# Small edits to a sliding-window attention and long-convolution kernel: 16-bit sine reads, masks accumulated where they fall, another row order, copies by DMA

## The chip, the cores and the metric

One core of a Trainium2 chip. The metric is the device time of one execution in microseconds (us), as the median of several executions. The profiler's span, from first to last instruction, is some 1.8 us shorter than that time. A program on a single core has no second die to compare with, so a single run's state is judged only against other runs of the same kernel; all runs here were listed as fast, and only such runs are compared.

## The reference, cut to what matters

Four layers with residuals on x of 2048 positions by 512 channels, bf16: attention, long convolution, attention, convolution.

```python
def _A_ref(x, wqkv, wo):                 # H = 32 heads, Dh = 16, window W = 8, dilation 2
    idx  = pos[:, None] - off[None, :]   # off = 0, 2, ..., 14
    mask = idx >= 0
    logits = einsum("bhsd,bhswd->bhsw", q, k[idx]) * scale
    attn   = softmax(where(mask, logits, -1e9))
    return einsum("bhsw,bhswd->bhsd", attn, v[idx]) @ wo
def _B_ref(u, A, B, C, log_dt, Dskip):   # complex state of 128 per channel
    K = real(einsum("dn,dnl,dn->dl", C, exp(dt*A*l), dt*B))      # one filter per channel, length 2048
    return irfft(rfft(u) * rfft(K)) + u * Dskip
x = x + _A_ref(layernorm(x), ...)
x = x + _B_ref(layernorm(x), ...)        # and both once more
```

## The kernel before

It runs in stages, and engines are shared in each: power tables of exp(dt*A) and a table for B (DVE and ACT, to 60 us); tables for A, the filter products `pk` and the keys of layer 0 (60 to 130); logits of layer 0 (to 160); weighted sum of the values (to 223), in whose gaps the sine tables g and the permuted filter `k_perm` are made; first convolution (to 311); logits (to 349) and values (to 407) of the second attention; second convolution (to 465). The parts that matter here, with the names that the traces use: PE is TensorE, DVE VectorE, ACT ScalarE, POOL GpSimd; `A_pr` and `prod` are products of queries and keys for the logits, `ex` their exponential, `s` its sum over the window, `rs` the reciprocal of that sum, `attn` the weights, `pav` the products of weights and values, `po` their sum, `pq` a projection, and `pb` what the convolution's matmuls write. The schedule fixes the program's order for PE, DVE, ACT and the DMA queue, and not for GpSimd (`MAN` in the kernel):

```python
def linit(self, q):                       # a full mask ahead of the logits of four rows
    L = self.ps_l.tile([P, 4, W, H], F32, name="L")
    for j in range(2):
        nc.tensor.matmul(L[:, 2*j:2*j+2], lhsT=e0, rhs=maskrow[...512 columns...], start=True, stop=True)

for q, ft in slots:                       # logits; DVE multiplies, PE sums over channels
    mult(q, ft); ...; lsum(q, ft)
    if ft == 0 and q > 0: mx(q - 1); ...; sub_exp(q - 1)
    if ft == 1 and q > 0: recip(q - 1)    # DVE: sums s over ex; ACT: ln and exp
    if ft == 3 and q > 0: norm_p(q - 1)
for n in range(16):                       # values; events ("p", n) and ("o", n) carry side work
    pv_mult(n); ...; pv_sum(n); ...; out_proj(n - 1)

def build_g2(...):                        # sine tables g, four blocks h, two buffers
    def indices(h):                       # GpSimd
        gi[h] = tmp.tile([P, 2, 4, P], I32, name="g2_i", bufs=2)
        ... iota; tensor_scalar(gi[h][:, k], gi[h][:, k], p21, bias, mult, add)
    def wrap(h):                          # DVE: bitwise_and 8191
    def sines(h):                         # ACT Sin, then a DMA to g_dram
```

`k_part(h, j)` copies the filter from `k_rl` into `k_perm`; the DMA queue (SP) issues all loads and stores in program order. `v_ext` and `kT_ext` hold values and keys with a halo of earlier rows, which is copied from the block before, one partition down.

## Time and profile before

| | before |
|---|---|
| time, median of 3 | 467.31 us (466.93 to 468.07) |
| profiled span | 465.0 us |
| busy share PE / DVE / ACT | 77% / 87% / 71% |

The prediction shows the table by stage and the gaps that the change aims at. For the reading afterwards I use seven marks, each the start or end of one named group of instructions in the trace, so that a stage's length doesn't depend on how a window is cut: A, the last `pk` matmul ends; B, the first value product `pav` starts; C, the last output projection (`pq<-wop`) of layer 0 starts; D, the first `prod` of layer 1 starts; E, its first `pav`; F, the ten matmuls that keep PE warm before the second convolution start; and the end of the span.

### The profile page before, as it was taken

How to read it: one execution, taken by the hardware profiler on the slowest of the kernel's cores; microseconds unless marked ns; L12 is line 12 of the kernel's file. 1: busy time of each engine (PE TensorE's matmuls, PEld its weight loads, DVE VectorE, ACT ScalarE, POOL GpSimd, SP SyncE). 2: the span in 40 equal slices, each digit the busy share in tenths (PEclk: the TensorE clock that was granted, in tenths of full speed). 3: DMA queues.
4: the chain of work that ended last, by engine and by line, in shares of the span. 5: the costliest groups of instructions: out<-in, count | busy, mean ns of one | idle time of the engine just before them, and what ended most of it. 6: DMA issues, size and time to landing. Idle time of an engine off the chain costs nothing.

```text
span 465.0 us, 12705 instructions
## 1 busy us (share of the span) xinstructions
PE 359.3 (77%) x5463; PEld 269.0 (58%) x5500; DVE 405.1 (87%) x570; ACT 328.8 (71%) x548; POOL 35.1 (8%) x46
## 2 busy tenths in 40 slices
PE   1000064879899887999898898999997999996795
PEld 1000023566575565777687788555555787775784
DVE  7799996999989898899687988889889999879854
ACT  5999669675555436998799986774652669699833
POOL 2000103000070004100400000000000020000000
PEclk9999995999999989999999899999999999999989
DMA  8900810101111763282256540670022053116614
GB/s 217 391 13 2 89 45 1 43 10 22 50 16 27 196 218 99 70 313 120 92 206 234 201 162 23 171 239 1 2 80 80 3 204 161 38 56 207 204 47 137
DMA packets 57402, 52.21 MB, mean 112 GB/s; under 512 B 28829, under 2 KB 45826, under 8 KB 56066
## 3 DMA queue, kind: packets, MB, share of 16 engines
q1 hardware_dynamic: 57202, 51.27, 35.5%
q8 instruction: 43, 0.70, 0.7%
q10 hardware_dynamic: 144, 0.13, 0.2%
q14 instruction: 13, 0.11, 0.1%
HBM read 30.28 MB, written 13.24 MB: 94 GB/s over the span
## 4 chain that ended last, share of the span: by engine, by line
PE 50%; ACT 20%; DVE 16%; DMA 7%; issue 4%; SPq 2%; DVEq 0%; ACTq 0%
PE po L374 9%; PE pp L218 6%; PE pq L315 5%; PE pq L161 5%; PE pq L386 4%; PE L L271 4%; PE pk L1096 4%; DVE pav L366 3%; DVE t L746 3%; ACT a1s L684 3%; DMA kf_ring<-kf_dram 2%; PE pb L695 2%; ACT ws L1014 2%; ACT x_blk L135 2%; PE pb L702 2%
## 5 line engine op out<-in xcount | busy, mean ns | idle before, releaser
L366 DVE TENSOR_TENSOR pav<-attn,v_ext 128x4096 bf16<-128x4096 bf16 x32 | 72.8, 2283 | 0.0
L374 PE MATMUL po<-ident,pav 128*128 128x128 bf16 x1024 | 64.3, 222 | 5.0 <-DVE pav L366 4.8
L374 PEld LDWEIGHTS <-pav 128*128 128x128 bf16 x1024 | 60.3, 100 | 13.0 <-DVE pav L366 9.5
L264 DVE TENSOR_TENSOR prod<-qT,kT_ext 128x4096 bf16<-128x4096 bf16 x29 | 65.8, 2285 | 1.0 <-ACT qT L163 0.6
L204 PE MATMUL pt<-ident,x_blk 128*128 128x128 bf16 x64 | 5.6, 241 | 41.5 <-ACT x_blk L135 41.5
L780 PE MATMUL pb<-Wp,t 128*128 128x128 bf16 x256 | 31.8, 222 | 5.9 <-DVE t L746 4.8
L377 ACT CAST oT<-po 128x512 bf16<-128x512 f32 x32 | 18.6, 580 | 25.1 <-PE po L374 25.1
L1096 PE MATMUL pk<-B_t,A_t 128*64 128x84 bf16 (+1 forms) x512 | 25.4, 210 | 12.3 <-issue 9.3
L218 PE MATMUL pp<-xnT,kT_ext 128*128 128x512 bf16 x125 | 31.7, 396 | 3.9 <-ACT xnT L207 3.5
L271 PEld LDWEIGHTS <-prod 128*128 128x128 bf16 x928 | 27.2, 96 | 10.0 <-DVE prod L264 3.6
L765 ACT CAST ub<-pb 128x1024 bf16<-128x1024 f32 x32 | 31.8, 1040 | 1.1 <-DVE t L746 1.1
L781 PE MATMUL pb<-WpJ,t 128*128 128x128 bf16 x256 | 31.4, 222 | 1.5 <-DVE t L746 1.5
L1096 PEld LDWEIGHTS <-A_t 128*64 128x64 bf16 (+1 forms) x512 | 23.1, 110 | 15.6 <-issue 12.3
L702 PE MATMUL pb<-a1s,w_sb 128*128 128x64 bf16 x768 | 30.3, 197 | 1.9 <-ACT ub L765 1.4
L386 PE MATMUL pq<-wop,oT 128*128 128x512 bf16 x112 | 30.6, 388 | 0.8
L317 ACT CAST v_ext<-pq 128x512 bf16<-128x512 f32 x32 | 18.7, 586 | 15.8 <-PE pq L315 15.5
L315 PE MATMUL pq<-wv,xnT 128*128 128x512 bf16 x119 | 29.5, 379 | 0.4
L161 PE MATMUL pq<-xnT,kT_ext 128*128 128x512 bf16 x120 | 29.3, 379 | 0.5 <-issue 0.3
L702 PEld LDWEIGHTS <-w_sb 128*128 128x128 bf16 x768 | 26.6, 100 | 5.1 <-issue 2.5
L271 PE MATMUL L<-ind,prod 128*128 128x8 bf16 x928 | 27.5, 166 | 2.3 <-DVE prod L264 2.1
L204 PEld LDWEIGHTS <-x_blk 128*128 128x128 bf16 x64 | 4.5, 108 | 42.9 <-ACT x_blk L135 42.4
L684 ACT CAST a1s<-pb 128x1024 bf16<-128x1024 f32 x28 | 27.4, 1025 | 2.1 <-PE pb L695 1.9
(224 smaller groups left out, 869.7 us busy)
## 6 DMA issues: line engine op xcount, KB each, us to landing
w_sb<-w_dram SPq DMA_DIRECT2D x8, 1024.0 KB
w_dram<-w_zero SPq DMA_DIRECT2D x1, 4096.0 KB
kf_ring<-kf_dram SPq DMA_DIRECT2D x16, 256.0 KB
kf_ring<-kf_dram SPq DMA_DIRECT2D x32, 128.0 KB
v_ext<-v_ext SPq DMA_DIRECT2D x4, 784.0 KB
x_blk<-in_A_x_dram SPq DMA_DIRECT2D x4, 512.0 KB
kT_ext<-in_A_wqkv_dram SPq DMA_DIRECT2D x4, 512.0 KB
x_sb<-in_A_x_dram SPq DMA_DIRECT2D x4, 512.0 KB
```

What stands on the lines that cost most here:

```text
L161: nc.tensor.matmul(pq[:], lhsT=self.wqk[:, dt, ft * P:(ft + 1) * P], rhs=self.xnT[:, dt, q * 512:(q + 1) * 512], start=(dt == 0), stop=(dt ...
L218: nc.tensor.matmul(pp[:], lhsT=self.wqk[:, dt, D + ft * P: D + (ft + 1) * P], rhs=self.xnT[:, dt, b * 512:(b + 1) * 512], start=(dt == 0), ...
L264: nc.vector.tensor_tensor(pr, self.qT[q][:, ft].unsqueeze(1).to_broadcast([P, W, 4, P]), kap, ALU.mult)
L271: self.nc.tensor.matmul(L[:, al, w, ft * 8:(ft + 1) * 8], lhsT=pr[:, w, al, :], rhs=self.c["ind8"][:], start=False, stop=True, skip_group_ ...
L315: nc.tensor.matmul(pp[:], lhsT=xnT[:, dt, a * P:(a + 1) * P], rhs=wv[:, dt, :], start=(dt == 0), stop=(dt == NDT - 1))
L366: nc.vector.tensor_tensor(pv[:], attn[:, n % 4].unsqueeze(2).to_broadcast([P, W, DH, H]), vap, ALU.mult)
L374: nc.tensor.matmul(po[:, ft, :], lhsT=pvf[:, w, ft * P:(ft + 1) * P], rhs=ident[:], start=(w == 0 and ft == 0), stop=(w == W - 1), skip_gr ...
L386: nc.tensor.matmul(pw[:], lhsT=oT[:, ftp, :], rhs=wo[:, ftp, :], start=False, stop=(ftp == NDT - 1))
L684: (nc.scalar.copy if eng == "act" else nc.vector.tensor_copy)(dst, src)
L702: nc.tensor.matmul(p2[:, j, :], lhsT=self.w2[:, ec * EC + j, :], rhs=a1s[:, ec * EC + j, :], start=True, stop=True)
L765: nc.scalar.copy(ub[:], p2)
L1096: nc.tensor.matmul(o, lhsT=lhs, rhs=Bt[:, ri, c * CH + ql].rearrange("p b g -> p (b g)"), start=(not half and j % 4 == 0 and ri == 0), sto ...
```

## The change

It takes DVE and ACT work away (integer wraps before the sines, casts and copies that a DMA can do), gives each sine index table memory of its own so that GpSimd no longer waits for a buffer between two tables, and reorders: statistics of block 1 into an idle stretch of ACT, masks after the logits and only where they fall, the reciprocal one slot later, value row 2 ahead of row 1. The core of the diff:

```diff
@@ mask
-        for j in range(2):
-            nc.tensor.matmul(L[:, 2 * j:2 * j + 2], lhsT=self.c["e0"], rhs=...to_broadcast([1, 2, W, H]), start=True, stop=True)
+    def mask(self, q):                         # called after the last lsum of q
+            a = q * 4 + 2 * j; w0 = a // 2 + 1
+            if w0 < W: matmul(L[:, 2 * j:2 * j + 2, w0:], ..., start=False, stop=True)
@@ core
-            projs += [(v_proj, a) for a in vs[6:]] + [(q_proj, 3, 0), (q_proj, 3, 1)]
+            projs += [(v_proj, a) for a in vs[6:]]
-                if ft == 1 and q > 0:
+                if ft == 2 and q > 0:
                     recip(q - 1)
+            q_proj(3, 0); q_proj(3, 1)
+            rows = [0, 2, 1, *range(3, NA)]
-                if n in (0, 2, 4, 6):
+                if n in (1, 2, 4, 6):
                     mult(3, n // 2)
@@ key halos, powers
+        if ext == "dma":
+            for t in range(NDT):
+                nc.sync.dma_start(self.kT[:, t, e0:e1, 1:P], self.kT[:, t, e0 + 16:e1 + 16, 0:P - 1])
-                    nc.scalar.copy(Pw[:, :, k - 3, 3, :], cv[:, 1])
+                    nc.sync.dma_start(Pw[:, :, k - 3, 0, :], Pw[:, :, k - 3, 1, :])
@@ build_g2: full-scale 16-bit angles, low half read in place, no wraps, borrowed memory
-        gi[h] = tmp.tile([P, 2, 4, P], I32, name="g2_i", bufs=2)
-    def wrap(h): nc.vector.tensor_scalar(gi[h][:], gi[h][:], 8191, None, ALU.bitwise_and)
+    own = tmp.tile([P, 2, 8 * P], I32, name="g2_i")
+    gi = [own[:, 0], own[:, 1], *(room[:, (2 + h) * 16 * P:(3 + h) * 16 * P].bitcast(I32) for h in range(2))]
+        gs = room[:, h * 8 * P:(h + 1) * 8 * P]            # room is the k_perm tile, not yet filled
+        nc.scalar.activation(gs, low16(gi[h]), ACT.Sin, scale=s8)
@@ statistics of block 1
             ln_a(0, "act")
+            stats(1, "act")
...
             front(0)
-            stats(1, "act")
@@ events
-              ("m", 0, 3): [G(gx, 0), G(gx, 1)],
+              ("m", 0, 3): [G(gx, h) for h in range(4)],
```

Left out: the twiddle tables of the second kind, which get the same 16-bit reading, and DVE's small index operations, which move from the start into later gaps, and a few moves of single loads.

## The prediction

> **What bounds the kernel now.** I read the chain of waits by engine first, then a table of busy time by stage, then each engine's instructions in order of time with the idle time before them. The shares by engine, from the page:
>
> ```profile
> PE 50%; ACT 20%; DVE 16%; DMA 7%; issue 4%; SPq 2%; DVEq 0%; ACTq 0%
> ```
>
> No engine owns the span, so a saving must be judged by stage. The table has start:end, length, then busy us of PE, PEld, DVE, ACT, POOL, the granted clock, DMA share and GB/s:
>
> ```profile
> 0.00:60.00 60.00, 5.12 (x37) 3.65 (x38) 52.96 (x117) 49.18 (x81) 4.36 (x16) 1.00 0.55 138
> 60.00:124.00 64.00, 46.96 (x534) 30.99 (x536) 59.31 (x98) 46.56 (x84) 5.16 (x3) 0.92 0.12 31
> 124.00:160.00 36.00, 35.42 (x586) 23.59 (x592) 31.41 (x26) 19.48 (x33) 9.38 (x8) 1.00 0.25 61
> 160.00:223.00 63.00, 56.16 (x746) 43.04 (x751) 57.14 (x55) 44.55 (x94) 6.87 (x9) 0.95 0.50 163
> 310.00:350.00 40.00, 39.52 (x499) 22.62 (x507) 34.18 (x28) 22.18 (x40) 0.00 (x0) 1.00 0.17 49
> 350.00:410.00 60.00, 56.51 (x794) 43.09 (x800) 56.85 (x61) 37.44 (x91) 2.90 (x1) 1.00 0.28 101
> ```
>
> To 60 us (powers and B table) DVE and ACT are both nearly full; to 124 (A tables, products, keys) DVE again, with a PE/ACT chain; 124 to 160 and 310 to 350 (logits) are PE's; the value stages (160 to 223, 350 to 410) hold PE and DVE nearly level. The two long convolution stages (223 to 310, 410 to 465) are not touched. The gaps that the change aims at, in order of time:
>
> ```profile
> 23.06 0.63 ACT L1022 CAST pow_t<-sq_z 128x512 bf16<-128x512 f32 x1
> 42.67 0.69 DVE L594 TENSOR_SCALAR w_qi<-w_qi 128x1024 int32<-128x1024 int32 x1
> 56.05 2.93 ACT L135 ACTIVATE x_blk<-x_blk,ln_nb,ln_rstd 128x512 bf16<-128x512 bf16 x4 [3.47 <-DVE ln_nb L125]
> 72.40 0.16 DVE L110 SCALAR_TENSOR_TENSOR ln_msq<-ln_s 128x4 f32<-128x4 f32 x1 [2.69 <-ACT ln_junk L80]
> 153.70 0.42 DVE L343 TENSOR_TENSOR s<-ex 128x512 bf16<-128x512 bf16 x1 [2.19 <-ACT ex L337]
> 182.71 0.69 DVE L634 TENSOR_SCALAR g_i<-g_i 128x1024 int32<-128x1024 int32 x1 [1.38 <-POOL g_i L631]
> 182.40 1.06 ACT L638 ACTIVATE g_s<-g_i 128x1024 bf16<-128x1024 int32 x1 [2.61 <-DMA g_dram<-g_s]
> 329.55 0.42 DVE L343 TENSOR_TENSOR s<-ex 128x512 bf16<-128x512 bf16 x1 [2.14 <-ACT ex L337]
> ```
>
> And the DMA queue's own issues ahead of the first value rows:
>
> ```profile
> 130.65 18.11 SPq L1114 DMA_DIRECT2D kd_dram<-kgs  x24
> 152.06 0.60 SPq L410 DMA_DIRECT2D v_ext<-rows  x1
> 152.70 0.66 SPq L320 DMA_DIRECT2D v_ext<-v_ext  x1
> ```
>
> The even value rows are ready at 147.1 (the eighth v_ext cast), but their halo copy is issued at 152.70, since the queue is busy from 130.65 on. It lands at 158.9 in the chain; the first value product (pav) starts at 159.7.
>
> **What the Trainium skill says.** "ScalarE: Activation LUTs", section "What ACT_TABLE_LOAD costs", gives an ACTIVATE with immediate operands 186 ns + 0.833 ns per column, and about 93 ns of overlap back to back. For 512 columns that is 613 ns, some 0.52 us apart; the trace has 0.63 us and 0.51 to 0.53 us spacing, so it agrees, and each removed pow_t cast is worth 0.51 us of ACT. "SBUF — State Buffer", "SBUF: two separate sides", says that the port pair shared by VectorE and GpSimd is an exclusive lock. The trace shows only POOL stretched (its g_i pair takes 4.52, 2.88, 1.63 and 2.24 us), while DVE's 4096-column products beside it keep 2.28. So moving all index work early on POOL should not slow DVE. "TensorE: Matmul & The Clock Gate", Part 1, says PE drops to half clock after about 3.4 us of idleness. After a waiting stretch one po group of 32 here took 3.56 us instead of 1.96, so a PE bubble costs a little twice.
>
> **The change part by part.**
>
> *To 62 us.* The twenty small DVE operations between 4.77 and 7.17 us move away from the start. The first ws product then waits only for the transposed A_im and the exponential (both near 6.0), gain 1.15. They return later as 1.6 us inside a stretch without DVE gaps. The removed casts free 5 x 0.51 = 2.5 us of ACT, but DVE paces those steps (its work runs unbroken from 20.5 to 40.1), so this is not gained. ACT's index work before the tenth squaring, with the f_t pair now there, is 3.2 instead of 2.6 us, and I keep DVE's 0.8 us gap there. The bit masks go: 42.40 to 43.44, 1.04 us. Sum for DVE at 45 us: about -0.5; ACT about +0.4.
>
> *62 to 130 us.* Before, ACT idled 3.47 us before normalising block 0, then ran the statistics of block 1 (6.05 us) after its keys. Now these statistics fill the idle time. ACT: 47.0 + 5.9 + 6.05 puts block 0 at 58.95 instead of 56.05; + 11.07 for keys + 6.05 for block 2 gives block 1 normalised from 76.05 instead of 79.06, gain 3.0. DVE loses its gaps of 2.69 and 0.59 us and three halo copies (0.34 + 0.60 + 0.60), so it stays ahead. The chain from 79 to 123 alternates ACT and PE and keeps the 3.0. The two mask matmul pairs (1.02 us) and the 0.67 us wait for the last key eviction no longer stand before the last products, about 1.5 more. The last products end near 125.4 instead of 129.9: -4.5.
>
> *130 to 160 us.* Moving the reciprocal one slot later lets DVE skip its waits of 1.47 and 2.19 us, and two query projections (2 x 0.86) leave the path ahead of the last logits. But the halo copy of the even rows still follows 24 kd_dram issues and the wop loads: it comes 28.3 us after the last products, as before. So DVE could start at 151.5 and waits to about 154.5. Gain at the first pav: 5.2, not 8. Order 0, 2, 1, 3 keeps the odd copy (landing near 159.5) off the path, since row 1 comes third.
>
> *160 to 223 us.* DVE loses four wraps (4 x 0.60) and the waits for POOL (2 x 1.38) and for k_rl (0.20): 5.4 us. ACT's waits for the g_dram writes (2.61 + 0.73 + 0.23) go too, but lie beside that. PE's work is 16 x 2.87 for the rows + 3.2 logits + 1.7 projections + 0.9 = 51.7 us, DVE's now 53.7, and PE ends 4.6 after DVE's last product. So DVE's saving passes through: -10.6 at 213.
>
> *310 to 410 us.* The same reordering of the core, with no crowded DMA queue. DVE's gaps of 2.14 and 2.08 vanish, the last logits come 1.73 + 0.55 us earlier (projections, mask columns), then the maximum waits some 0.9 us for them: net -3.1. The masks shrink from 4096 to 1792 columns per layer; by their 0.53 us per pair that is about 1.0 us of PE, partly counted above.
>
> Sum: 467.3 - 10.6 - 3.1 = 453.6. I add 1.4 for coupling between three nearly full engines and half-clock PE after the new wait for v_ext: **455.0 us**.
>
> **The rivals.**
>
> *The DMA queue becomes the wall.* Some 17 more issues (5 powers, 12 key halos) go in order through one queue, each half a us or so. If the key halos of block 2, queued after 24 kd_dram issues, land late, DVE's first logits product waits. At that estimate they land near 118 to 120 against a DVE arrival of 117.3, while PE takes its logits only at 125, so it should be hidden. If v_ext is late as well, 4 us are given back: 459. For it: the v_ext reading above. Against it: nothing new stands between kd_dram and v_ext.
>
> *PE was the bound all along in the logits and value stages.* PE is 98% and 94% busy there, and removing DVE work then does nothing: only the K stage (4.5), the mask columns (2) and the moved projections count, some 458 to 460. For it: the chain is PE's from 207 to 223 and from 357 to 405. Against it: in 160 to 223 PE waited on DVE's pav and on x_sb (2.31 us), and DVE had no slack.
>
> *The statistics fill delays block 0.* Keys of block 0 come 2.9 us later; if the products are held by that instead of by ACT's later work, the K stage gains only about 1.5 and the total is 458.
>
> *Better than the sum.* If ACT's freed 2.5 us do shorten the power steps, and PE keeps up: 450.
>
> **Range and chances.** The rivals put the weak side at 458 to 460 and the strong side at 450; I set 449.5 to 460.5. The 2% line is 458.0. The sum lies 3 us under it after the correction, and two of the three adverse rivals cross it only together: faster 0.78, same 0.21, slower 0.01.
>
> **What would show it.** In the changed profile: no idle before ACT's first x_blk, and none near the second block's ln_msq; the last pk matmuls ending near 125; the first pav near 154.5, behind a v_ext landing rather than behind DVE work; no g_i wraps on DVE, and g_s sines without a DMA wait; the first pb near 213; DVE without waits for ex in both logits stages; layer 1 shorter by about 3 us from first logits to its first pb; the convolution stages unchanged within 0.5 us. The prediction is wrong if DVE waits for kT_ext halos or k_rl, if pav starts later than 157, or if PE's groups in the value stages slow down.

## The result, and the profile after

| | before | changed |
|---|---|---|
| time, median of 4 | 467.12 us (466.77 to 468.07) | 455.42 us (454.86 to 456.39) |
| ratio | | 0.9749 (95%: 0.9725 to 0.9773) |
| profiled span | 465.0 us | 453.2 us |

A ratio here is the mean time of one kernel's fast runs over that of the other's of the same rounds, so it isn't quite the ratio of the medians. The total is where it was predicted. Whether the steps are is another question, and the marks answer it. "Control" is the changed kernel once more, run beside the experiments; the predicted column takes the prediction's own steps.

| stage | before | changed | control | control less before | predicted |
|---|---|---|---|---|---|
| start to A (powers, tables, keys) | 129.87 | 126.28 | 124.95 | -4.9 | -4.5 |
| A to B (logits, layer 0) | 29.83 | 28.41 | 28.42 | -1.4 | -0.7 |
| B to C (values, layer 0) | 62.74 | 59.85 | 59.87 | -2.9 | -5.4 |
| C to D (convolution 1) | 88.89 | 89.17 | 88.83 | -0.1 | 0 |
| D to E (logits, layer 1) | 37.92 | 35.12 | 35.12 | -2.8 | -3.1 |
| E to F (values, layer 1) | 57.58 | 58.20 | 57.88 | +0.3 | 0 |
| F to the end (convolution 2) | 58.17 | 56.17 | 55.53 | -2.6 | 0 |

Two columns of one kernel differ too: the first stage by 1.3 us. The cause stands in the trace. Here is the second half of block 0's `pk` products in the changed kernel's first profile (start, us, engine, line, operation, names, shapes, count, idle before):

```profile
78.66 5.03 PE L1111 MATMUL pk<-B_t,A_t 128*128 128x84 bf16 x64 [0.60 <-ACT kgs L1115]
```

and in the control:

```profile
79.47 2.91 PE L1111 MATMUL pk<-B_t,A_t 128*128 128x84 bf16 x64 [1.36 <-ACT kgs L1115]
```

The same 64 matmuls of the same program run at nearly half speed in one execution and at full speed in the other: the granted clock was 0.50 over the first 5.03 us and 1.00 over the 2.91 us of the control. In the first profile PE had stood idle for 3.52 and 1.29 us ahead of the two groups before, in the control for 2.79 and 0.77; the sixth experiment's profile has 3.51 and 1.29 and 5.03 us again. Such stretches fall differently in each execution. The last stage, whose code no edit touches, took from 55.33 to 59.47 us in the runs below. Start, length, busy us of PE, PEld, DVE, ACT, POOL, clock, DMA share and GB/s of that stage, first in the control, then in the slowest of the runs (the seventh experiment):

```profile
395.07:450.60 55.53, 43.69 (x848) 39.07 (x847) 41.09 (x56) 39.37 (x46) 0.00 (x0) 0.97 0.44 137
```

```profile
396.83:456.30 59.47, 46.45 (x848) 41.45 (x847) 41.18 (x56) 39.37 (x46) 0.00 (x0) 0.91 0.42 128
```

DVE and ACT do the same work in the same time; PE is 2.8 us busier at a clock of 0.91. So the -2.6 of the last row is no gain of the change, and anything under 2 us is read from stage lengths that don't meet such stretches: A to B and D to E repeat to 0.02 us between profiles of the same code.

The stages of the changed kernel, cut as near as possible as before:

```profile
58.00:120.00 62.00, 48.42 (x538) 33.17 (x543) 58.48 (x97) 43.53 (x74) 4.74 (x3) 0.92 0.20 43
120.00:155.00 35.00, 34.68 (x597) 23.43 (x600) 34.44 (x26) 19.65 (x33) 25.16 (x16) 1.00 0.30 72
155.00:216.00 61.00, 56.05 (x773) 42.43 (x780) 56.53 (x54) 45.70 (x96) 2.67 (x4) 1.00 0.56 178
303.00:340.00 37.00, 36.58 (x497) 21.75 (x504) 34.23 (x27) 20.66 (x37) 0.00 (x0) 1.00 0.15 44
```

In the logits stage of layer 0 DVE is now full (34.44 of 35.00 us), and POOL is busy for 25.16 us instead of 9.38. The lines behind that, and those that answer to the gaps shown of before:

```profile
119.14 2.29 DVE L273 TENSOR_TENSOR A_pr<-qT,kT_ext 128x4096 bf16<-128x4096 bf16 x1 [1.99 <-PE pq L162]
137.39 0.83 DVE L354 TENSOR_TENSOR s<-ex 128x512 bf16<-128x512 bf16 x1
138.26 0.66 DVE L356 TENSOR_TENSOR s<-s 128x256 bf16<-128x256 bf16 x1
...
154.09 0.68 DVE L367 TENSOR_TENSOR attn<-ex,rs 128x1024 bf16<-128x1024 bf16 x1
154.69 2.29 DVE L377 TENSOR_TENSOR pav<-attn,v_ext 128x4096 bf16<-128x4096 bf16 x1
...
193.58 0.43 DVE L1256 COPY k_perm<-k_rl 128x1024 bf16<-128x1024 bf16 x1 [2.36 <-DMA g_dram<-k_perm]
...
325.52 0.69 DVE L367 TENSOR_TENSOR attn<-ex,rs 128x1024 bf16<-128x1024 bf16 x1 [0.54 <-ACT rs L361]
```

The wait for `ex` before the sum `s` is gone in both layers, and so are the wraps. But the sums in layer 0 now take 0.83 and 0.66 us, where before they took 0.43 and 0.29. The first `pav` follows DVE's own work without idle time, so no landing of `v_ext` holds it. And a wait stands at 193.58 that before didn't have: a copy into `k_perm` waits for a write from the same memory to `g_dram`. The DMA queue's issues show why it lands so late:

```profile
188.54 0.56 SPq L650 DMA_DIRECT2D g_dram<-k_perm  x1
```

Its sine table was ready at 179.8, but the write stands behind 18 loads of `k_rl` (from 177.27 on), is issued at 188.54, and ends, in the chain of waits, 4.95 us later. A third thing is new in PE's order. The compiler put 16 pairs of the first convolution's matmuls ahead of the products that this copy holds up, though the source has them after the output projections. The rest of that kind starts only at 216.24. The first of these 32 matmuls:

```profile
193.92 0.24 PE L706 MATMUL pb<-F1c,k_perm 128*64 128x128 bf16 x1
```

Theories at this point. First: the value stage lost 2.4 of its 5.4 us to the new `k_perm` wait, and DVE's saving otherwise passes through. Rival: PE bounds the value stage, and the wait is idle time that costs nothing. Second: GpSimd's work beside DVE doubles the small sums, and that holds back the first `pav`. Rival: the copy of the even `v_ext` rows does, as I had predicted.

### The profile page after: what moved, and what is told of

The parts are those of the page before. It is cut to its first block, busy times and chain, and to the rows that moved or that the text cites.

```text
span 453.2 us, 12714 instructions
## 1 busy us (share of the span) xinstructions
PE 354.9 (78%) x5459; PEld 268.0 (59%) x5498; DVE 402.2 (89%) x558; ACT 326.0 (72%) x543; POOL 44.5 (10%) x46
## 4 chain that ended last, share of the span: by engine, by line
PE 52%; ACT 20%; DVE 16%; DMA 7%; issue 3%; SPq 1%; DVEq 0%; ACTq 0%
PE po L385 9%; PE pp L219 6%; PE pq L326 6%; PE pq L162 5%; PE L L280 5%; PE pq L397 4%; PE pk L1111 4%; DVE t L757 4%; DVE pav L377 3%; ACT a1s L695 3%; DMA v_ext<-v_ext 3%; PE pb L713 2%; PE pb L706 2%; ACT ln_junk L86 2%; ACT ln_junk L81 2%
## 5 line engine op out<-in xcount | busy, mean ns | idle before, releaser
L385 PEld LDWEIGHTS <-pav 128*128 128x128 bf16 x1024 | 58.6, 98 | 13.0 <-DVE pav L377 9.4
L385 PE MATMUL po<-ident,pav 128*128 128x128 bf16 x1024 | 62.5, 219 | 4.8 <-DVE pav L377 4.8
L119 POOL TENSOR_TENSOR ln_rstd<-ln_rstd,ln_mh 128x4 f32<-128x4 f32 x6 | 10.0, 1658 | 229.0 <-DVE ln_rstd L118 207.0
L1111 PE MATMUL pk<-B_t,A_t 128*64 128x84 bf16 (+1 forms) x512 | 27.0, 217 | 6.8 <-issue 3.5
L280 PEld LDWEIGHTS <-prod 128*128 128x128 bf16 x928 | 27.3, 96 | 7.4 <-DVE prod L273 1.5
L1111 PEld LDWEIGHTS <-A_t 128*64 128x64 bf16 (+1 forms) x512 | 24.7, 115 | 10.0 <-issue 5.9
L397 PE MATMUL pq<-wop,oT 128*128 128x512 bf16 x110 | 29.3, 379 | 0.9
```

The costliest lines, as they stand in the source:

```text
L280: self.nc.tensor.matmul(L[:, al, w, ft * 8:(ft + 1) * 8], lhsT=pr[:, w, al, :], rhs=self.c["ind8"][:], start=(ft == 0 and w == 0 and al % ...
L385: nc.tensor.matmul(po[:, ft, :], lhsT=pvf[:, w, ft * P:(ft + 1) * P], rhs=ident[:], start=(w == 0 and ft == 0), stop=(w == W - 1), skip_gr ...
L397: nc.tensor.matmul(pw[:], lhsT=oT[:, ftp, :], rhs=wo[:, ftp, :], start=False, stop=(ftp == NDT - 1))
L1111: nc.tensor.matmul(o, lhsT=lhs, rhs=Bt[:, ri, c * CH + ql].rearrange("p b g -> p (b g)"), start=(not half and j % 4 == 0 and ri == 0), sto ...
```

## The experiments

Twelve kernels in three sets; each set shares its runs of the kernel before. Times are medians of 6 executions in the first eight, 4 in the others. Set 1 had 467.78 us for the kernel before, set 2 467.46, set 3 467.83. Each set ran on another chip, and only set 2 (experiments 5 to 8) has the control beside it, so medians of different sets are not compared closely.

### 1. The sine tables out of the way of the k_perm copies

```diff
-    gi = [own[:, 0], own[:, 1], *(room[:, (2 + h) * 16 * P:(3 + h) * 16 * P].bitcast(I32) for h in range(2))]
+    gi = [own[:, 0], own[:, 1], *(room[:, h * 16 * P:(h + 1) * 16 * P].bitcast(I32) for h in range(2))]
-        gs = room[:, h * 8 * P:(h + 1) * 8 * P]
+        gs = room[:, (32 + h * 8) * P:(40 + h * 8) * P]
```

> Edit: in the changed kernel the finished sine tables move to the upper half of the long-filter tile, and the two borrowed index buffers to the lower half, so that the copies of the first half of k_perm no longer overwrite a sine table whose write to g_dram is still under way. Theory A (this wait is what ate a part of the gain in the value stage of layer 0): the 2.36 us idle of DVE before the k_perm copy at 193.6 goes to below 0.3; the changed kernel gains 2.4 less what the compiler's order had put into the hole (32 pairs of the convolution's first matmuls, some 0.9 us, which now stand after the out projections again), so 1.0 to 1.6 us: 453.8 to 454.4. Rival B (PE is the bound in that stage, or DVE meets another wait at once): 455.0 to 455.6, and 0.9 us later at the first pb.

Measured: 453.87 us (450.49 to 455.87), ratio 0.9712 (0.9671 to 0.9752). The copy no longer waits:

```profile
189.42 0.42 DVE L1256 COPY k_perm<-k_rl 128x1024 bf16<-128x1024 bf16 x1
...
212.45 1.23 DVE L695 CAST a1s<-pb 128x1024 bf16<-128x1024 f32 x1 [3.65 <-PE pb L706]
```

B to C is 57.41 us instead of 59.87: 2.46 less, the whole wait. Against before it is 5.33 less, where the prediction's step had 5.4. But with this placement the compiler puts the 16 pairs (not 32, as I had written) back behind the output projections, and DVE then waits 3.65 us for the first of them. C to D was 89.63 here, and 90.15 to 92.18 in the other three kernels of this order; with the matmuls in the hole it was 88.15 to 89.49 in nine profiles. So one stage gains 2.4, the next takes 2.0 more on the mean (90.7 against 88.7), and the median of the whole doesn't part from the control's. Why the next stage is longer is not shown. The kernel before has the same order and the same wait of 3.65 us, and took 88.89; and PE's stretches at half clock don't part them, as the control has two in that stage and the seventh experiment, with 92.18, one. Theory A stands for the stage; for the total, its 1.0 to 1.6 us are not shown.

### 2. Three index tables placed later

```diff
-              ("m", 0, 3): [G(gx, h) for h in range(4)],
+              ("m", 0, 3): [G(gx, 0)], ("p", 0): [G(gx, h) for h in range(1, 4)],
```

> Edit: three of the four GpSimd index tables move from the logits stage to the first value row. Theory A (GpSimd work beside them doubles the small DVE operations): the two sums over ex in layer 0's logits stage go from 0.83 and 0.66 us back to 0.42 and 0.29, DVE is ready for the first value product near 152.8 instead of 154.7, and then waits some 2 us for the copy of the even v_ext rows, which lands near 154.7; total 455.4 within 0.5. Rival B (GpSimd does not stretch DVE; the doubled times have another cause): 0.83 and 0.66 stay, no wait for v_ext. Rival C (the copy lands early): first pav near 152.8 and 2 us gained, 453.4.

Measured: 453.46 us (452.12 to 456.30), ratio 0.9718 (0.9681 to 0.9756). Nothing moved: POOL's first index operation still starts 0.1 us after A, the sums keep 0.83 and 0.66, A to B is 28.42. That first operation does wait, and for the last `pk` product, as it did in the kernel before:

```profile
124.59 1.18 POOL L644 IOTA g_i<- 128x512 int32 x2 [20.83 <-PE pk L1111]
```

The fifteen behind it then run one after the other without idle time. With memory of their own nothing later holds them, and GpSimd has no other instruction between, so a place later in the program doesn't make them start later. The experiment tested nothing; the sixth and the twelfth mend it.

### 3. The even value rows copied ahead of the last filter writes

```diff
+                        if c == NCH - 1 and g == 3:
+                            la.kd_late.append(lambda dst=dst, sr=sr: nc.sync.dma_start(dst, sr)); continue
                         nc.sync.dma_start(dst, sr)
...
-        ev = {("v", 1): [x_load],
+        ev = {("v", 0): [lambda: [f() for f in la.kd_late]], ("v", 1): [x_load],
```

> Edit: the last six of the 24 kd_dram writes are issued after the copy of the even v_ext rows instead of before it. Theory A (DVE, stretched by GpSimd, is ready only at 154.7, so the copy is not what the first value product waits for): the copy is issued near 145.9 instead of 147.6, first pav stays at 154.7, total 455.4 within 0.5. Rival B (the copy is the gate, as I predicted): first pav near 153 and 1.5 us gained, 453.9. If the six late writes delay k_rl, a wait of k_perm copies for k_rl shows, and up to 2 us are lost.

Measured: 453.93 us (452.60 to 458.57), ratio 0.9727 (0.9679 to 0.9774). The copy is issued at 143.13, 18.9 us after A instead of 21.3, and has landed by 148.9, 3.7 us ahead of the first `pav`, and A to B is 28.42 as in the changed kernel. Rival B, my predicted gate, falls: 2.4 us of earlier issue are worth nothing.

### 4. The three together

The edits of 1, 2 and 3.

> Edit: the three edits before together. Theory A (two things, the copy of the even rows and DVE stretched by GpSimd, hold the first value product at the same instant; each alone gives nothing, both together 2 us): first pav near 152.8, and the total lower than that of the first edit alone by 1.5 to 2.0 us, 452.0 to 452.8. Rival B (PE bounds the value stage, so an earlier start is eaten up): no more than 0.5 us below the first edit alone.

Measured: 453.32 us (451.15 to 456.45), ratio 0.9713 (0.9672 to 0.9753). A to B 28.42, B to C 57.41, as in the first. As the second edit did nothing, this says no more than 1 and 3 do.

### 5. The control

The changed kernel, unedited.

> The changed kernel itself, once more, as the control for the runs beside it (the four edits of the first set spread by 2 to 6 us from execution to execution on that chip). Theory (part of the first profile is chance: PE ran 64 matmuls of the first block's products in 5.03 us instead of 2.91): the last products end near 124.5 instead of 126.3; from there to the first value product again 28.4 us; from there to the last output projection 59.9 us; logits to value in layer 1 35.1 us; total 453.5 to 456. Rival (the first profile is typical): the products end at 126.3 again.

Measured: 454.94 us (452.38 to 456.67), ratio 0.9721 (0.9677 to 0.9764). A at 124.95, A to B 28.42, B to C 59.87, D to E 35.12. The late A of the first profile was the slow stretch of PE.

### 6. Index tables held back by one-column copies

```diff
+    def gate(h):
+        nc.vector.tensor_copy(gi[h][:, 0:1], p21)
-              ("m", 0, 3): [G(gx, h) for h in range(4)],
+              ("m", 0, 3): [G(gx, 0)], ("m", 1, 3): [G(gg, 1), G(gx, 1)], ("m", 2, 3): [G(gg, 2), G(gx, 2), G(gx, 3)],
```

> Edit: as the second run wished, which changed nothing since GpSimd has nothing to wait for and started at the same point; now one-column copies by DVE into the index buffers hold the second and third table back until both pairs of doubled sums have run. Theory A (GpSimd doubles small DVE operations beside it): sums over ex back to 0.42 and 0.29 at both places, DVE ready 1.5 to 2.0 us earlier; from the end of the last products to the first value product 26.5 to 27.0 us instead of 28.4, if the copy of the even v_ext rows has landed by then, else a wait of DVE for v_ext and 28.4 as before. Rival B: 0.83 and 0.66 stay.

Measured: 454.30 us (452.41 to 457.93), ratio 0.9715 (0.9670 to 0.9759). The compiler pulled index operations of later tables ahead of the held one, so GpSimd was still busy at the first pair of sums. At the second pair it wasn't, and the two pairs can be held side by side within one execution. GpSimd:

```profile
137.70 0.85 POOL L645 TENSOR_SCALAR k_perm<-k_perm,aux 128x512 int32<-128x512 int32 x1
...
145.67 4.84 POOL L645 TENSOR_SCALAR g_i<-g_i,aux 128x512 int32<-128x512 int32 x1
151.57 0.56 POOL L644 IOTA k_perm<- 128x512 int32 x1 [1.06 <-DVE k_perm L653]
```

and DVE's second sums:

```profile
138.03 0.66 DVE L356 TENSOR_TENSOR s<-s 128x256 bf16<-128x256 bf16 x1
...
150.81 0.29 DVE L356 TENSOR_TENSOR s<-s 128x256 bf16<-128x256 bf16 x1
```

The sum at 138.03 starts inside GpSimd's operation of 137.70 to 138.55 and takes 0.66 us; that at 150.81 starts in GpSimd's pause (150.51 to 151.57) and takes 0.29. It supports theory A, though A to B shrank by 0.25 only.

### 7. Held-back tables, early copy and the upper half

The edits of 1, 3 and 6.

> Edit: held-back index tables, early copy of the even v_ext rows, and the sine tables in the upper half, together. Theory A: products to first value product 26.4 to 26.9 us without a wait for v_ext; from there to the last output projection 57.4 us as in the first run; total 1.5 (value stage less the hoisted matmuls) + 1.5 to 2.0 below the control, near 451.5 to 452.5. Rival B (PE-bound value stage): the earlier start is eaten, the value stage takes 59 us.

Measured: 455.08 us (453.07 to 458.11), ratio 0.9726 (0.9682 to 0.9771). A to B 28.17, B to C 57.83 (its first `pav` took 2.70 us, beside GpSimd). No version of these beats the changed kernel in the total by more than the executions spread.

### 8. The statistics of block 1 back in their old place

```diff
             ln_a(0, "act")
-            stats(1, "act")
...
             front(0)
+            stats(1, "act")
             stats(2, "act")
-        tables(0, {2: [lambda: ln_a(1, "act")], 3: [lambda: ln_b(1)]})
+        tables(0, {3: [lambda: ln_a(1, "act")], 4: [lambda: ln_b(1)]})
```

> Edit: the statistics of the second block go back behind the keys of the first, as in the kernel before. Prediction's step (block 1 is normalised 3.0 us earlier and the chain keeps it): ACT idles some 3 us before the first block, the second block is normalised near 78, the last products end 3.0 us later than in the control (4.5 if all of the stage's gain hangs on it), total +3. Rival (PE and DVE are ahead anyway, the gain of the stage is DVE's start, the masks and the projections): +0 to +1.

Measured: 456.69 us (454.04 to 459.01), ratio 0.9774 (0.9727 to 0.9821). ACT's idle time is back, and the second block follows:

```profile
55.25 2.94 ACT L136 ACTIVATE x_blk<-x_blk,ln_nb,ln_rstd 128x512 bf16<-128x512 bf16 x4 [2.84 <-DVE ln_nb L126]
...
77.28 2.92 ACT L136 ACTIVATE x_blk<-x_blk,ln_nb,ln_rstd 128x512 bf16<-128x512 bf16 x4
```

In the control the two stand at 58.76 and 75.89. The second block is 1.39 us later than there, and A, at 126.34, is 1.39 us later too. From block 1 to A it is 49.06 us in both, so the chain keeps every bit, as predicted. But block 1 itself stands between 74.86 and 75.89 in the ten profiles whose code is the same up to A, so the reordering is worth 1.4 to 2.4 us, not 3.0. It lies between the two theories. The wait before the `k_perm` copy was absent in this one profile (B to C 57.66), and I don't know why: DVE came later to it by 1.39 us against the control, its `g_dram` write was issued only 0.44 later, and had landed at most 4.2 us after that instead of 5.6. In the other profiles with this wait the landing took from 3.3 to 5.4 us, so it varies by more than the difference.

### 9. The reciprocal back one slot

```diff
-                if ft == 2 and q > 0:
+                if ft == 1 and q > 0:
```

> Edit: the reciprocal of the sum over ex goes back one slot, as in the kernel before. Prediction's step (its move removes two DVE waits for ex, but only part of that counts in layer 0 since a v_ext landing holds the first value product there): the waits of some 1.5 and 2.2 us return in both layers; from the end of the last products to the first value product in layer 0 28.4 to 29 us. Theory now (DVE alone paces the logits stage of layer 0, no landing does): both waits count in full, less what of the GpSimd work they let pass: 31 to 32 us. In layer 1 from the first logits product to the first value product 35.1 becomes 37 to 38 us under both. Total +4 to +6 or +2 to +3.

Measured: 455.93 us (454.04 to 458.65), ratio 0.9752 (0.9690 to 0.9815). One wait of the two is back in layer 0, both in layer 1 (1.62 and 1.49 us):

```profile
134.96 0.43 DVE L354 TENSOR_TENSOR s<-ex 128x512 bf16<-128x512 bf16 x1 [1.55 <-ACT ex L348]
...
147.77 0.41 DVE L354 TENSOR_TENSOR s<-ex 128x512 bf16<-128x512 bf16 x1
```

A to B is 29.35, 0.9 more; D to E is 36.61, 1.5 more. My later theory (31 to 32) missed: the second `ex` comes in time, since two products that GpSimd stretched (4.89 us the pair, and 2.69) gave ACT time. The prediction's 28.4 to 29 is nearer, for another reason than the one it gave.

### 10. Masks and query projections back ahead of the logits

```diff
+        for j in range(2): matmul(L[:, 2 * j:2 * j + 2], ... full mask ..., start=True, stop=True)   # in linit
-        if ft == NDT - 1: self.mask(q)
+            projs += [(v_proj, a) for a in vs[6:]] + [(q_proj, 3, 0), (q_proj, 3, 1)]
-            q_proj(3, 0); q_proj(3, 1)
```

> Edit: full mask matmuls ahead of the logits, and the two query projections ahead of the last logits, as before. Prediction's step (1.0 to 1.7 us ahead of the last products; in layer 1 the last logits 1.73 + 0.55 us later): the last products end 1.0 to 1.7 us later than in the control (near 126.2); layer 1 logits to value 36.5 to 37.3 instead of 35.1. Rival (DVE paces layer 1's logits stage too, and PE's order does not matter): 35.1 stays, total +1.0 to +1.7 only.

Measured: 457.77 us (455.23 to 458.56), ratio 0.9777 (0.9729 to 0.9825). The four mask matmuls stand ahead of the last products again, 1.02 us after a wait of 0.67:

```profile
102.69 5.77 PE L1113 MATMUL pk<-B_t,A_t 128*128 128x84 bf16 x128
...
119.36 5.78 PE L1113 MATMUL pk<-B_t,A_t 128*128 128x84 bf16 x128
```

A is at 125.14, only 0.2 later than in the control, but A doesn't decide here: in this profile block 1 was normalised at 73.84, 1.0 to 2.1 us ahead of the ten profiles named in experiment 8, in code that the edit doesn't touch. The stretch between the starts of the last two groups of products, which holds the masks, took 16.67 us, as in the kernel before (16.64), and 14.87 to 14.89 in the twelve other profiles: 1.8 more, and the expectation was 1.0 to 1.7. A to B is 28.88, 0.5 more. D to E is 37.78, 2.7 more than 35.12 and all but the whole difference from before (37.92).

### 11. Four wraps back on DVE, and key halos back on DVE

On the kernel of experiment 1.

```diff
+    def wrap(h): nc.vector.tensor_scalar(gi[h], gi[h], 65535, None, ALU.bitwise_and)
+    ("p", 1): wrap 0, ("p", 3): wrap 1, ("p", 4): wrap 2, ("p", 5): wrap 3
-            if b < 3: la.front_ext(b, "dma")
+    la.front_ext(0..2, "dve") inside the tables of the blocks after
```

> Edit on the kernel of the first run (sine tables in the upper half): four integer wraps of 0.6 us are put back on DVE in the value stage of layer 0, and the key halos of the first three blocks go back to DVE copies; the two act in different stages. Theory A (DVE is the bound of that value stage once the k_perm wait is gone): 57.4 us from the first value product to the last output projection becomes 59.6 to 60.0. Rival B (PE is): 57.4 to 58.0. Halos: the wait of DVE ahead of its first logits product goes, and the last products still end near 124.7 within 0.4, since that wait was beside PE's products; if DVE's 1.5 us more count, 126.

Measured: 455.62 us (455.14 to 456.49), ratio 0.9743 (0.9704 to 0.9781). B to C is 59.79, 2.38 more than the 57.41 without the wraps: four times 0.60 us of DVE pass through undiminished. Rival B, PE as the bound of the value stage, falls. DVE's wait ahead of its first logits product is gone, and A, at 123.95, is if anything earlier (49.04 us after block 1, as in the control): copying the halos by DMA gained nothing there. But A to B grew from 28.42 to 29.38 as DVE came later, so at B the copies by DMA are worth 1.0 us.

### 12. No multiply-adds on GpSimd

Its output is wrong, which doesn't matter for the time. Relative error 0.118: the sines get unscaled indices, all else is the same.

```diff
-            nc.gpsimd.tensor_scalar(g, g, p21, bias, ALU.mult, ALU.add)
```

> Edit: the changed kernel without the eight multiply-adds of GpSimd on the index tables (the result is wrong on purpose; the sine tables hold other angles, all else is the same). Theory A (GpSimd's work beside them is what doubles DVE's small sums): both sums back to 0.42 and 0.29 at both places, the one stretched product back to 2.28, and from the end of the last products to the first value product 26.4 to 26.6 us; or 27 to 28 with a wait of DVE for v_ext, if the copy of the even rows lands later than that. Rival B (something else doubles them): 28.4 stays.

Measured: 453.23 us (450.51 to 454.40), ratio 0.9681 (0.9632 to 0.9730). DVE in the logits stage of layer 0:

```profile
135.89 0.42 DVE L354 TENSOR_TENSOR s<-ex 128x512 bf16<-128x512 bf16 x1
136.34 0.29 DVE L356 TENSOR_TENSOR s<-s 128x256 bf16<-128x256 bf16 x1
...
139.63 0.69 DVE L367 TENSOR_TENSOR attn<-ex,rs 128x1024 bf16<-128x1024 bf16 x1 [0.46 <-ACT rs L361]
...
147.97 0.42 DVE L354 TENSOR_TENSOR s<-ex 128x512 bf16<-128x512 bf16 x1
148.43 0.29 DVE L356 TENSOR_TENSOR s<-s 128x256 bf16<-128x256 bf16 x1
...
151.46 0.69 DVE L367 TENSOR_TENSOR attn<-ex,rs 128x1024 bf16<-128x1024 bf16 x1 [0.22 <-ACT rs L361]
152.07 2.29 DVE L377 TENSOR_TENSOR pav<-attn,v_ext 128x4096 bf16<-128x4096 bf16 x1
```

Every doubled sum is back to its old time, both times, and the stretched product too. That settles theory A: GpSimd's work was the cause. Two times (0.41 + 0.37) and 0.42 are 1.98 us of DVE; A to B is 27.30, only 1.1 less, since DVE now reaches `attn` before ACT has the reciprocal and waits 0.46 and 0.22. The first `pav` starts without a wait for `v_ext` even here, which is the last word on that gate. Whether the 1.1 us reach the total is not shown: B to C took 60.83 in this profile, 0.96 more than in the control. There the third `pav` waits 0.29 us for the odd `v_ext` rows, and PE runs at half clock from 163.43 to 166.84, which it doesn't in the control's value stage.

## Why the prediction was right or wrong

The total was right: 455.0 predicted, 455.42 measured. The mechanisms were not all right. The value stage gained 2.5 us less than its step said. Against that stand the correction for coupling (1.4) and the second convolution, where no edit acts and the prediction gave nothing, which was 2.0 us shorter in the first profile and 2.6 in the control. So part of the hit is luck.

**To 62 us.** Right in kind and nearly in size. The first `ws` product starts at 6.19 instead of 7.17, a gain of 0.98 for 1.15. ACT's freed casts turned into waits for DVE (0.90, 1.24, 0.61 and 0.41 us ahead of four squarings), as the step said.

**62 to 130 us.** Right: -4.9 in the control for -4.5, and nearly so part by part. Block 1 was normalised at 75.89 in the control and 75.09 in the first profile, for 76.05 predicted and 79.06 before. The statistics alone are worth 1.4 to 2.4 us of that (experiment 8) and not 3.0; without their move block 1 still comes 1.8 us earlier than before, of which block 0's earlier start (55.25 instead of 56.05) is 0.8, and the runs don't separate the rest. From block 1 to A the control gains another 1.75 us, and the masks ahead of the last products are worth 1.8 (experiment 10) for about 1.5 predicted. The key halos gain nothing up to A (experiment 11).

**130 to 160 us.** The size was off by 0.7 us (-1.4 against -0.7) and the mechanism wrong. The step said that the first `pav` stands "behind a v_ext landing rather than behind DVE work". I had read the landing at 158.9 from the chain of waits of before and not DVE's own lines beside it:

```profile
154.69 4.49 DVE L264 TENSOR_TENSOR prod<-qT,kT_ext 128x4096 bf16<-128x4096 bf16 x2
159.10 0.68 DVE L356 TENSOR_TENSOR attn<-ex,rs 128x1024 bf16<-128x1024 bf16 x1
159.70 2.28 DVE L366 TENSOR_TENSOR pav<-attn,v_ext 128x4096 bf16<-128x4096 bf16 x1
```

DVE is busy without a gap from 154.69 into the `pav`: the copy had landed at 158.9, 0.8 us before the `pav` started, and still the chain named it. (The "28.3 us after the last products" doesn't come out of these lines: 158.9 less 129.9 is 29.0, and it is 29.0 that gives the 154.5.) Experiment 3 shows that an earlier copy gains nothing, and experiment 12 that a `pav` 1.1 us earlier doesn't meet it. Counted from A, the prediction had 26.1 us for DVE alone (125.4 to 151.5). Measured were 28.4, and 27.3 without GpSimd's multiply-adds (experiment 12), of which 0.68 are waits for the reciprocal. So what held the `pav` back is the next step.

**"Moving all index work early on POOL should not slow DVE."** This step failed. DVE lost 1.98 us in the logits stage to GpSimd, 1.1 of it on the path from A to B. I had reasoned from before's trace, where only GpSimd was stretched; but there the small sums never met it (at 139.89 GpSimd had ended at 139.77, and at 153.70 it was idle). The page that I named, "SBUF — State Buffer", section "SBUF: two separate sides", says of the shared port pair that "the other fully blocks", whichever began first. The lock works in both directions, and I had taken one. The trace of experiment 6 agrees: the sum that began at 138.03, inside GpSimd's operation, ended at 138.69, 0.14 us after that one (138.55).

**160 to 223 us.** The mechanism was right and the term was mis-sized by a wait that I had not seen. DVE's 5.4 us do pass through: 5.33 are there once the `k_perm` copies are free (experiment 1), and four wraps put back cost 2.38 of 2.40 (experiment 11). The other 2.95 stand against the two waits for POOL (2.76); the wait of 0.20 for `k_rl` stayed. So PE's two stretches at half clock in the value stage of before (3.41 us each), a rival for this gain, leave at most 0.2 us of it. But in the changed kernel the sine tables lie in `k_perm`'s memory, and the fourth one's write stands behind 18 `k_rl` loads in the queue. The copy waits 2.36 us for it, and the stage gains 2.9 instead of 5.4. The diff and the queue's issues of before held all that was needed to see it: the write after the second `k_rl` batch, at some 0.6 us an issue. The prediction asked only whether DVE would wait for `k_rl`.

**310 to 410 us.** -2.8 for -3.1, all of it in the logits stage, as said. The two causes overlap: undone alone, the order on PE costs 2.7 us and the reciprocal 1.5, and both together were 2.8 in the kernel before. The step expected no crowding for `v_ext` in this layer. Yet in 8 of the 13 profiles after the change the third `pav` waits 0.16 to 1.15 us for the odd rows, which the new row order asks for; before it never did. E to F shows no gain or loss that follows this wait.

**The correction of 1.4 us** for coupling stood in for the wait of 2.4 that I had not named. That the total came out with it is luck.

**The rivals.** The DMA queue as the wall came true, though at another place than the rival said: neither key halos nor `v_ext`, but `g_dram`. PE as the bound all along is refuted by experiment 11 for the value stage of layer 0. And a sign that I had set up as fatal, "DVE waits for kT_ext halos", appeared: seven profiles name that copy for 0.2 to 1.6 us ahead of DVE's first logits product (the first changed profile puts its 1.99 us down to a query projection that ended at about the same time). It cost nothing, as that wait lies beside PE's last products, which end 7 us after it. The remark on the chances doesn't fit the rivals' own numbers: 459, 458 to 460 and 458 each reach the line of 458.0 alone.

**Untouched stages.** The first convolution kept its length (-0.1). The second was 2.6 shorter in the control, but its spread among runs of the same code is 4.1 us, so none of this is credited to the change.

## What to carry to other kernels

When a buffer is lent to something else, look up where its last reader stands in the DMA queue, and count the issues ahead of it: a wait moves from the removed work to the memory that was lent. Memory of its own also lets an engine start as early as it can, and for GpSimd that may be just where VectorE is the bound. A chain of waits names one of two events that lie close together, so read the engine's own lines beside it before calling something the gate; and where executions spread more than an edit is worth, compare the length of the stage between two named instructions and not the total. Put both marks close around the edit: in experiment 10 a mark counted from the start of the span hid 1.6 of 1.8 us.

## What the Trainium skill lacked or had wrong

- "SBUF — State Buffer", section "SBUF: two separate sides": right that the lock blocks both sides, but the sizes that the page has (DVE 6.8 and GpSimd 1.5 times slower) come without shapes. Here a DVE sum of 512 bf16 columns went from 0.42 to 0.83 us, one of 256 from 0.29 to 0.66, and a 4096-column product from 2.28 to 2.70 once among several, while GpSimd's 512-column integer multiply-add took 0.68 us at its quickest and 4.89 at its slowest. So here long DVE products held GpSimd up, and short DVE sums paid.
- "TensorE: Matmul & The Clock Gate", Part 1: has the idle window, says that it is free-running, and that the matmuls at half clock differ in number between runs, but gives this for a kernel's start only. Here it fell in mid-kernel: the same 64 matmuls took 2.91 or 5.03 us, and an untouched stage, 55.3 to 59.5 us long, was granted 0.91 to 0.99 of the clock.
- No page that I read tells that the compiler can move matmuls of a later stage ahead on PE: 16 pairs stand at 193.92 in the changed kernel, and ahead in the same way in the seven edited kernels with the sine tables in the lower half of `k_perm`, but in none of the four with them in the upper half.
